# Inverting the 32 by 32 triangles of the first three time blocks as two 16 by 16 ones

## The chip, the cores and the metric

The kernel runs on one core of one Trainium2 chip. The number looked at is the device time of one execution in microseconds (us). Before the change it is 1301.52 us, the median of 3 runs that went from 1301.41 to 1301.69.

## The reference

A recurrence over 768 steps for 4 batches of 8 heads, each with a 40 by 40 state, feeds two dense layers. Its output for a step, one row per batch and step, is the input x of the layers.

```python
for t in range(S):                                   # S = 768, per batch and head
    y[:, :, t] = einsum('bhd,bhde->bhe', rt, state)
    Sa = einsum('bhde,bhe->bhd', state, at)
    state = state * wt[:, :, None, :] - einsum('bhd,bhe->bhde', Sa, bt)
    state = state + einsum('bhd,bhe->bhde', vt, kt)
x = y as (3072, 320)
h = x @ w_in;  x = (max(h, 0) + alpha * min(h, 0)) @ w_out          # 320 -> 2048 -> 320
g = x @ w_gate;  out = (silu(g) * (x @ w_val)) @ w_out2             # 320 -> 1536 -> 320
```

## The kernel before

The 768 steps are cut into 6 time blocks `m` of 128 steps, each of two chunks of 64. Within a chunk the recurrence becomes matrix products, for which a 64 by 64 unit lower triangular matrix has to be inverted for every batch, pair of heads and chunk. For one time block these are 32 triangles per 32 partitions; they lie in the tile `tt` (two tiles, used in turn by even and odd blocks).

The work has these parts. `prep_a` and `prep_b` make, batch by batch, the factors of a chunk (tiles `Wx`, `AN`, `kbt`, `KB`) and the triangles. `inverse(m)` inverts all triangles of block m. `seq` is the recurrence itself, chunk by chunk and batch by batch, two batches side by side; its first product that needs the inverse is `pp` (L731), and its multiplication by the mask is L751. `conv` turns one weight tile into 32-bit halves: three instructions on DVE (L177 to L179), one on ACT (L180), POOL's L186 and L187, a cast on ACT (L191), POOL's L192, and a store to `wd`. Its tile `wy` has one buffer, so the next tile's L177 waits for the L187 of the one before. There are 32 such tiles for the first dense layer (`c1`) and 36 for the second (`c2`). `mlp1` is the first dense layer of one time block, fed by fetches `wt<-wd`; the second layer follows at the end.

`inverse(m)` halves the 64 by 64 triangle. The two 32 by 32 diagonal blocks are inverted by forward substitution in 31 steps: each multiplies a column by a row into `tmp` (L614) and subtracts it from the rows below (L622). For the first block these columns are split in three parts, one on POOL and two on DVE; for the others in two parts on DVE. Then come two transposes on DVE (L626 into `tn`, L628 into `tt`), a product on PE (`eps`, L636), copies on ACT, and a second product (`dps`, L655) that gives the off-diagonal 32 by 32 quarter.

The order on each engine is not that of the code: a scheduler that runs when the program is built sets it, from priorities that `drive` gives as it steps several generators in proportion (`N_INV` is the number of steps that it counts for an inversion). `narrow` asks it to put POOL's L186 after the last POOL instruction of an inversion that has been recorded so far (`mark["pool"]`), where there is one. Each engine then runs its list strictly in that order, so an instruction that waits holds up all behind it.

## Time and profile before

| | us |
|---|---|
| median of 3 runs | 1301.52 |
| profiled execution, time | 1305.71 |
| profiled execution, span from first to last instruction | 1304.0 |
| PE busy | 1115.3 |
| DVE busy | 799.9 |
| ACT busy | 595.1 |
| POOL busy | 409.5 |

The profiled execution is 4.19 us longer than the median and has 1.71 us outside its span. Engines are PE (matrix products; PEld is its weight loads), DVE, ACT, POOL, and SP, which issues most transfers. Busy times add over stages with different limits, so the rows further down are taken by stage.

### The profile page before, as it was taken

To read this page: it belongs to the slowest core of one execution; us is meant where nothing else is said; L and a number is where in the kernel's file an instruction comes from. 1 tells how busy PE (TensorE), PEld (TensorE's weight loads), DVE (VectorE), ACT (ScalarE), POOL (GpSimd) and SP (SyncE) were. 2 spreads that over 40 slices of the span, in tenths; PEclk is the share of its full clock that TensorE was granted. 3 is DMA by queue.
4 is the path that set the end of the run, shared out by engine and by line. 5 is a ranking of instruction groups with operands and counts; after the bars stand their busy time and mean duration, and the time that the engine had idled before them with its cause. 6 is when DMAs were issued, how large, how long until landed. Compare 5 with 4: busy or idle time off the path is not lost.

```text
span 1304.0 us, 24772 instructions
## 1 busy us (share of the span) xinstructions
PE 1115.3 (86%) x9056; PEld 940.2 (72%) x9056; DVE 799.9 (61%) x1713; ACT 595.1 (46%) x1463; POOL 409.5 (31%) x604
## 2 busy tenths in 40 slices
PE   3522777969899988989699969999999999999998
PEld 3521667856687776777577757877888888888887
DVE  7999678899769876986987754333332323232222
ACT  4731665645673586477555453333322222222222
POOL 9886656645421353156426540000000000000000
PEclk9765779989989998999899989999999999999999
DMA  5321468876645565466648857785700000000000
GB/s 162 118 72 43 130 194 267 261 231 217 219 142 166 159 223 168 137 195 202 195 137 266 265 193 223 215 307 202 282 25 21 25 21 17 21 1 21 10 11 21
DMA packets 101128, 188.54 MB, mean 145 GB/s; under 512 B 13712, under 2 KB 43664, under 8 KB 101008
## 3 DMA queue, kind: packets, MB, share of 16 engines
q1 hardware_dynamic: 92848, 183.03, 44.1%
q10 hardware_dynamic: 8160, 3.93, 1.1%
q8 instruction: 72, 1.18, 0.4%
q14 instruction: 48, 0.39, 0.1%
HBM read 150.22 MB, written 36.70 MB: 143 GB/s over the span
## 4 chain that ended last, share of the span: by engine, by line
PE 46%; DVE 26%; DMA 12%; ACT 7%; issue 4%; POOL 3%; SPq 1%; ACTq 0%; DVEq 0%; POOLq 0%
PE pg L235 10%; PE pv L235 10%; PE u L235 5%; DMA wt<-wd 5%; DVE la L622 4%; DVE tmp L614 3%; PE o L946 3%; PE o L947 3%; PE o L945 3%; DVE AN L515 2%; PE gp L748 2%; DVE g L275 2%; PE mnp L540 2%; DMA raw_wa<-in_wa_dram 2%; DVE rest L498 2%
## 5 line engine op out<-in xcount | busy, mean ns | idle before, releaser
L191 ACT CAST gh<-g 128x512 fp32r<-128x512 f32 (+1 forms) x176 | 105.7, 600 | 184.8 <-DVE g L965 124.8
L965 DVE TENSOR_TENSOR g<-pv,sg 128x512 f32<-128x512 f32 x72 | 49.8, 692 | 227.4 <-PE pv L235 224.5
L192 DVE TENSOR_TENSOR gl<-g,gh 128x512 fp32r<-128x512 f32 (+1 forms) x176 | 123.3, 700 | 89.9 <-ACT gh L191 89.3
L235 PE MATMUL u<-xh,wt 128*128 128x512 f32 (+1 forms) x416 | 150.0, 403 | 18.8 <-DVE g L275 15.8
L275 DVE SCALAR_TENSOR_TENSOR g<-g,neg,u 128x512 f32<-128x512 f32 (+1 forms) x104 | 72.8, 700 | 71.0 <-ACT g L274 70.8
L186 POOL TENSOR_SCALAR wz<-wz 128x384 f32<-128x384 f32 (+1 forms) x68 | 79.4, 1168 | 102.6 <-ACT wz L180 74.5
L235 PEld LDWEIGHTS u<-xh,wt 128*128 128x128 f32 x416 | 79.8, 195 | 42.3 <-DVE g L275 21.8
L540 PE MATMUL mnp<-AN,kbt 128*128 128x128 f32 x384 | 67.1, 335 | 50.5 <-DVE AN L515 28.3
L963 ACT ACTIVATE sg<-pg 128x512 f32<-128x512 f32 x72 | 43.1, 599 | 139.7 <-PE pg L235 139.7
L274 ACT ACTIVATE g<-u 128x512 f32<-128x512 f32 (+1 forms) x104 | 58.8, 566 | 103.2 <-PE u L235 74.6
L235 PE MATMUL pg<-xh,wt 128*128 128x512 f32 x288 | 101.5, 392 | 0.0
L540 PEld LDWEIGHTS mnp<-AN,kbt 128*128 128x128 f32 x384 | 61.6, 244 | 54.3 <-issue 24.9
L235 PE MATMUL pv<-xh,wt 128*128 128x512 f32 x288 | 100.4, 389 | 0.0
L192 POOL TENSOR_TENSOR wc<-wz,wc 128x384 fp32r<-128x384 f32 (+3 forms) x84 | 80.8, 969 | 56.6 <-ACT wc L191 49.7
L946 PE MATMUL o<-wt,gh 128*128 128x320 f32 x288 | 87.7, 308 | 0.0
L241 PE MATMUL d<-gl,wt 128*128 128x512 f32 (+1 forms) x208 | 82.3, 398 | 6.1 <-DVE gl L192 5.8
L945 PE MATMUL o<-wt,gh 128*128 128x320 f32 x288 | 87.2, 308 | 0.0
L622 DVE TENSOR_TENSOR la<-la,tmp 128x120 f32<-128x120 f32 (+37 forms) x304 | 84.6, 307 | 1.4
L614 DVE TENSOR_TENSOR tmp<-la 128x120 f32<-128x120 f32 (+37 forms) x304 | 82.9, 300 | 2.5 <-POOL la L589 0.8
L235 PE MATMUL u<-xl,wt 128*128 128x512 f32 (+1 forms) x208 | 81.1, 390 | 1.7 <-DVE xl L192 1.7
L242 PE MATMUL d<-gh,wt 128*128 128x512 f32 (+1 forms) x208 | 78.6, 380 | 0.0
L240 PE MATMUL d<-gh,wt 128*128 128x512 f32 (+1 forms) x208 | 70.0, 397 | 8.8 <-ACT gh L191 6.7
(117 smaller groups left out, 2730.0 us busy)
## 6 DMA issues: line engine op xcount, KB each, us to landing
wt<-wd SPq DMA_DIRECT2D x128, 384.0 KB
wt<-wd SPq DMA_DIRECT2D x116, 320.0 KB
wd<-wc SPq DMA_DIRECT2D x40, 384.0 KB
raw<-in_moe_w_out_dram SPq DMA_DIRECT2D x28, 320.0 KB
wd<-wc SPq DMA_DIRECT2D x28, 320.0 KB
raw_wa<-in_wa_dram SPq DMA_DIRECT2D x48, 160.0 KB
raw_bk<-in_bk_dram SPq DMA_DIRECT2D x48, 160.0 KB
raw<-in_moe_w_in_dram SPq DMA_DIRECT2D x16, 256.0 KB
```

Of the source, the lines that this page charges most:

```text
L186: nc.gpsimd.tensor_scalar(f, f, LEAST, None, ALU.is_ge)
L191: nc.scalar.copy(out=h, in_=raw)
L192: eng.tensor_tensor(out=l, in0=raw, in1=h.bitcast(F32), op=ALU.subtract)
L235: nc.tensor.matmul(ps, lt, rh, start=(i == 0), stop=(i == len(ops) - 1))
L241: nc.tensor.matmul(ps, wh, gl, start=False, stop=False)
L242: nc.tensor.matmul(ps, wl, gh, start=False, stop=last)
L275: nc.vector.scalar_tensor_tensor(g, g, neg[:, f:f + 1], ps, ALU.mult, ALU.add)
L540: nc.tensor.matmul(ps[:, s].rearrange("p h t -> p (h t)"), kbt[:, g * SH + s].rearrange("p j t -> p (j t)"), an[:, :, g * SH + s, :],)
L614: eng.tensor_tensor(out=tv, in0=ml[:, r0:r1, kk:kk + 1].to_broadcast([128, nr, ns]), in1=tl[:, kk:kk + 1, c0:c1].to_broadcast([128, nr, ns ...
L622: last = eng.tensor_tensor(out=dst, in0=dst, in1=tv, op=ALU.subtract)
L945: nc.tensor.matmul(ops[q], gh[:, ts], wh, start=first, stop=False)
L946: nc.tensor.matmul(ops[q], gh[:, ts], wl, start=False, stop=False)
```

## The change

For blocks 0, 1 and 2 (`LASTB = 2`) `inverse` now calls `blocked`; the others call `substitute`, which is the former code of the blocks after the first. `blocked` inverts the two 16 by 16 diagonal triangles of each 32 by 32 one side by side, in 15 steps of two products and two subtractions, all on DVE. The remaining 16 by 16 quarter is made of two products on PE: `ups`, then a copy `us` on ACT, then `yps`, subtracted from `tt` on DVE. This takes three transposes in place of two: into `dn`, into `tt`, and from `tt` into `tn`. The number of steps that `drive` counts is 29 for these blocks. POOL has no part in any inversion now, so `mark["pool"]` is never set.

```diff
+QUART = 16
+LASTB = 2
+    def blocked(m, mc, ml, tl):
+        tt = mc
+        for kk in range(QUART - 1):
+            tvs = []
+            for o in (0, QUART):
+                nr, ns = QUART - 1 - kk, kk + 1
+                tmp = (mac_p if m else bp).tile([128, QUART * QUART // 4], F32, tag=f"tmp{min(o, 1)}", name="tmp")
+                tv = tmp[:, 0:nr * ns].rearrange("p (a b) -> p a b", a=nr)
+                rows, cols = slice(o + kk + 1, o + QUART), slice(o, o + kk + 1)
+                nc.vector.tensor_tensor(
+                    out=tv,
+                    in0=ml[:, rows, o + kk:o + kk + 1].to_broadcast([128, nr, ns]),
+                    in1=tl[:, o + kk:o + kk + 1, cols].to_broadcast([128, nr, ns]),
+                    op=ALU.mult,
+                )
+                tvs.append((tv, tl[:, rows, cols]))
+            for tv, dst in tvs:
+                mark["inv"] = nc.vector.tensor_tensor(out=dst, in0=dst, in1=tv, op=ALU.subtract)
+            yield
+        dn = scr(m, 0).rearrange("p (a b) -> p a b", a=NG)
+        nc.vector.transpose(out=dn.rearrange("p n s -> p s n"), in_=tl.rearrange("p t s -> p s t"))
+        yield
+        for g in range(2):
+            ups = (ps_b if m else bps).tile([128, NH, HALF], F32, tag="b" if m else f"s{2 + g}", name="ups")
+            for n in range(NH):
+                for q in range(4):
+                    nc.tensor.matmul(
+                        ups[32 * q:32 * q + 32, n, :],
+                        mc[32 * q:32 * q + QUART, g * NH + n, 0:HALF],
+                        dn[32 * q:32 * q + QUART, g * NH + n, :],
+                        tile_position=(32 * q, 32 * q),
+                    )
+            yield
+        mark["inv"] = nc.vector.transpose(out=tt[:, :, 0:HALF].rearrange("p n t -> p t n"), in_=tl)
+        yield
+        for g, ups in enumerate(upss):
+            us = (mac_p if m else bp).tile([128, NH, HALF], F32, tag="us", name="us")
+            nc.scalar.copy(out=us, in_=ups)
+            ...
+                    nc.tensor.matmul(
+                        yps[pr, n, :], us[pr, n, :], tt[pr, g * NH + n, QUART:HALF], tile_position=(32 * q, 32 * q),
+                    )
+            off = tt[:, g * NH:g * NH + NH, QUART:HALF]
+            mark["inv"] = nc.vector.tensor_tensor(out=off, in0=off, in1=yps, op=ALU.subtract)
+            yield
+        tn = scr(m, 0).rearrange("p (a b) -> p a b", a=NG)
+        mark["inv"] = nc.vector.transpose(out=tn, in_=tt[:, :, 0:HALF])
     def inverse(m):
...
+        if m > LASTB:
+            yield from substitute(m, ml, tl)
...
+        else:
+            tn = yield from blocked(m, mc, ml, tl)
-    N_PREP, N_INV, N_SEQ, N_MLP = 8, 40, 13, 2 * K1 + 4
+    def n_inv(m):
+        return 40 if m > LASTB else 29
```

How the order moves is shown at three places. The first is DVE's list where the first two inversions end. Before, the substitution of the second inversion (tiles `la_1344`, `tmp`) ends in its two transposes, and the first mask multiplication of `seq` follows at once.

```order
L179 SCALAR_TENSOR_TENSOR wy_1140<-raw_1136,wz_1141 128x384
L622 TENSOR_TENSOR la_1344<-la_1344,tmp_1839 128x10
L626 STREAM_TRANSPOSE la_1845<-la_1344 128x32x32
L628 STREAM_TRANSPOSE tt1_175<-la_1344 128x32x32
L751 TENSOR_TENSOR gs_1115<-gp_1375,mask_117 128x8x64
L177 TENSOR_SCALAR wy_1175<-raw_1173 128x320
```

Now DVE has there the transpose that ends the second substitution (L627, into `dn`), then the first inversion's transpose into `tt` (L642, tile `tt0_174`), and its two subtractions (L655) and last transpose (L658), with instructions of three weight tiles between them (L179 to L181 are the former L177 to L179).

```order
L627 STREAM_TRANSPOSE la_1802<-la_1493 128x32x32
L642 STREAM_TRANSPOSE tt0_174<-la_470 128x32x32
L179 TENSOR_SCALAR wy_1260<-raw_1256 128x384
L180 SCALAR_TENSOR_TENSOR wz_1261<-raw_1256,wy_1260 128x384
L181 SCALAR_TENSOR_TENSOR wy_1260<-raw_1256,wz_1261 128x384
L179 TENSOR_SCALAR wy_1300<-raw_1298 128x320
L180 SCALAR_TENSOR_TENSOR wz_1301<-raw_1298,wy_1300 128x320
L181 SCALAR_TENSOR_TENSOR wy_1300<-raw_1298,wz_1301 128x320
L655 TENSOR_TENSOR tt0_174<-tt0_174,yps_828 128x16x16
L179 TENSOR_SCALAR wy_1354<-raw_1350 128x384
L180 SCALAR_TENSOR_TENSOR wz_1355<-raw_1350,wy_1354 128x384
L181 SCALAR_TENSOR_TENSOR wy_1354<-raw_1350,wz_1355 128x384
```

Four more weight tiles stand between that L658 and the first mask multiplication (now L804); of the last of them, and of the second inversion's transpose into `tt1_175`, this is the end.

```order
L179 TENSOR_SCALAR wy_1518<-raw_1514 128x384
L180 SCALAR_TENSOR_TENSOR wz_1519<-raw_1514,wy_1518 128x384
L642 STREAM_TRANSPOSE tt1_175<-la_1493 128x32x32
L181 SCALAR_TENSOR_TENSOR wy_1518<-raw_1514,wz_1519 128x384
L804 TENSOR_TENSOR gs_1235<-gp_1502,mask_117 128x8x64
```

So 15 weight tiles stand ahead of the first mask multiplication where 9 stood before. The second place is PE's list there. Before, the last products of the preparations (`kbp`) are followed by `eps`, `dps` and the recurrence's `pp`.

```order
L568 MATMUL kbp<-ident,kbt 128x128 x4
L636 MATMUL eps<-la,tt_174 32x32 x64
L655 MATMUL dps<-tt_174,la 32x32 x64
L731 MATMUL pp<-tt_174,zs_166 64x64 x8
L731 MATMUL pp<-tt_174,zs_170 64x64 x8
L737 MATMUL pp<-ident,ut 128x128 x4
```

Now `ups` and `yps` of the first inversion (`tt_174`) stand ahead of `eps` (now L685), with most of the second inversion's `ups` (`tt_175`) among them.

```order
L570 MATMUL kbp<-ident,kbt 128x128 x4
L634 MATMUL ups<-la,tt_174 32x32 x128
L634 MATMUL ups<-la,tt_175 32x32 x35
L651 MATMUL yps<-tt_174,us 32x16 x64
L634 MATMUL ups<-la,tt_175 32x32 x26
L651 MATMUL yps<-tt_174,us 32x16 x64
L634 MATMUL ups<-la,tt_175 32x32 x44
L685 MATMUL eps<-la,tt_174 32x32 x64
L634 MATMUL ups<-la,tt_175 32x32 x8
L704 MATMUL dps<-tt_174,la 32x32 x64
L784 MATMUL pp<-tt_174,zs_166 64x64 x8
```

The first `pp` has moved behind 256 products of the first inversion and 113 of the second. The third place is DVE's list at the end of the third inversion (block 2, again `tt0_174`). Before, it is the substitution's last steps between instructions of `mlp1` (L275, L192) and of a weight tile.

```order
L614 TENSOR_TENSOR tmp_3918<-la_3291,la_3293 128x10
L179 SCALAR_TENSOR_TENSOR wy_2099<-raw_2095,wz_2100 128x384
L622 TENSOR_TENSOR la_3293<-la_3293,tmp_3918 128x10
L275 SCALAR_TENSOR_TENSOR g_3780<-g_3780,neg_76,u_3727 128x512
L626 STREAM_TRANSPOSE la_3924<-la_3293 128x32x32
L628 STREAM_TRANSPOSE tt0_174<-la_3293 128x32x32
```

Now the subtractions of the quarter come behind one chunk of the recurrence, and no weight tile stands near.

```order
L746 TENSOR_TENSOR ST3_182<-ST3_182,Wx_1222 128x4x40
L762 COPY gs_4072<-ST3_182 64x2x2x40 x2
L642 STREAM_TRANSPOSE tt0_174<-la_3694 128x32x32
L655 TENSOR_TENSOR tt0_174<-tt0_174,yps_4266 128x16x16
L277 SCALAR_TENSOR_TENSOR g_3763<-g_3763,neg_76,u_3728 128x512
L194 TENSOR_TENSOR gl_3767<-g_3763,gh_3766 128x512
L655 TENSOR_TENSOR tt0_174<-tt0_174,yps_4385 128x16x16
L658 STREAM_TRANSPOSE la_4462<-tt0_174 128x1024
```

Between the third inversion's first transpose (L586, now L665) and this end there were 9 weight tiles and 14 multiplications L275 before; there are 2 and 9 now. At the last chunk of the recurrence PE's list has 547 products of the first layer's second half (L240 to L246) where it had 576, and 70 groups of 8 of its first half where it had 72: this work now stands behind it.

## Rows read from the trace of the kernel before

**Rows 1.** Stages: start:end, length; busy us (instructions) by engine; PE clock; DMA.
```profile
45.40:142.00 96.60, 30.89 (x399) 28.52 (x398) 94.98 (x254) 39.63 (x107) 72.42 (x112) 0.59 0.24 79
120.40:142.00 21.60, 14.29 (x314) 12.92 (x315) 20.23 (x54) 11.83 (x26) 10.95 (x11) 0.50 0.27 87
142.00:240.00 98.00, 79.22 (x1025) 70.71 (x1023) 68.69 (x131) 64.69 (x191) 59.03 (x85) 0.85 0.66 211
240.00:320.00 80.00, 65.91 (x602) 53.90 (x601) 78.75 (x209) 38.37 (x112) 44.93 (x60) 0.96 0.76 243
320.00:800.00 480.00, 423.23 (x4438) 341.90 (x4436) 369.04 (x843) 281.45 (x731) 192.20 (x265) 0.95 0.61 191
800.00:907.00 107.00, 102.40 (x433) 80.51 (x434) 42.69 (x60) 36.59 (x62) 0.00 (x0) 1.00 0.78 253
907.00:1304.00 397.00, 391.32 (x2025) 343.91 (x2023) 110.45 (x161) 107.86 (x188) 0.00 (x0) 1.00 0.11 39
```

**Rows 2.** The chain that ends last, shares by line, from 45.4 to 142 us.
```profile
by line: DVE la L622 22.7%; DVE tmp L614 22.2%; issue 8.8%; DVE rest L498 6.8%; DVE AN L515 6.6%; DVE la L626 4.1%; DVE la L586 3.9%; DVE kbt L529 3.6%; DVE wz L178 3.4%; DVE wy L179 3.3%; DVE wy L177 2.7%; DVE tt L628 1.8%; DVE Wx L505 1.7
```

**Rows 3.** L614 alone by stage: DVE busy, then POOL busy.
```profile
45.40:142.00 96.60, 27.76 (x96) 15.14 (x31) 0.59 0.24 79
240.00:320.00 80.00, 16.70 (x52) 0.00 (x0) 0.96 0.76 243
```

**Rows 4.** L622 alone by stage, columns as in rows 3.
```profile
45.40:142.00 96.60, 27.83 (x96) 15.57 (x31) 0.59 0.24 79
240.00:320.00 80.00, 17.15 (x52) 0.00 (x0) 0.96 0.76 243
```

**Rows 5.** Groups by shape: xcount | busy us, mean ns of one | idle before.
```profile
L614 DVE TENSOR_TENSOR tmp<-la 128x21 f32<-128x21 f32 x10 | 1.9, 191 | 0.0
L614 DVE TENSOR_TENSOR tmp<-la 128x57 f32<-128x57 f32 x10 | 2.1, 209 | 0.0
L622 DVE TENSOR_TENSOR la<-la,tmp 128x60 f32<-128x60 f32 x11 | 3.6, 326 | 0.2
```

**Rows 6.** DVE in order of time: start us, us, instruction.
```profile
83.38 1.90 DVE L586 STREAM_TRANSPOSE la<-tt 128x1024 f32<-128x1024 f32 x1
...
120.36 1.96 DVE L626 STREAM_TRANSPOSE la<-la 128x1024 f32<-128x1024 f32 x1
...
141.84 0.65 DVE L751 TENSOR_TENSOR gs<-gp,mask 128x512 f32<-128x512 f32 x1
...
239.87 1.97 DVE L586 STREAM_TRANSPOSE la<-tt 128x1024 f32<-128x1024 f32 x1
...
317.27 2.21 DVE L626 STREAM_TRANSPOSE la<-la 128x1024 f32<-128x1024 f32 x1
```

**Rows 7.** PE in order of time: start us, us of all, xcount of weight-and-product pairs.
```profile
122.38 3.63 PE L636 MATMUL eps<-la,tt 32*32 32x32 f32 x128 [42.23 <-DVE la L626]
...
132.33 1.97 PE L731 MATMUL pp<-tt,zs 128*64 128x64 f32 x32 [1.18 <-POOL wc L192]
...
670.91 1.83 PE L636 MATMUL eps<-la,tt 32*32 32x32 f32 x102
```

**Rows 8.** A weight tile on DVE, in order of time.
```profile
130.51 0.33 DVE L177 TENSOR_SCALAR wy<-raw 128x320 uint32<-128x320 uint32 x1 [0.89 <-POOL wz L187]
...
135.88 0.36 DVE L177 TENSOR_SCALAR wy<-raw 128x384 uint32<-128x384 uint32 x1
...
137.45 0.55 DVE L179 SCALAR_TENSOR_TENSOR wy<-raw,wz 128x384 uint32<-128x384 uint32 x1
```

**Rows 9.** The same weight tile on POOL, in order of time.
```profile
138.73 1.17 POOL L186 TENSOR_SCALAR wz<-wz 128x384 f32<-128x384 f32 x1 [1.23 <-ACT wz L180]
139.99 1.00 POOL L187 TENSOR_TENSOR wz<-wz,wy 128x384 f32<-128x384 f32 x1
```

**Rows 10.** A piece of the chain in the first layer's last block: start, us.
```profile
816.01 1.83 PE u L235 x8
```

80 lines of the change are left out of this document (38 added, 42 removed).

## The prediction

> **What bounds the kernel now.** I read the stages first [rows 1]: which engine is full in each tells what a saved microsecond is worth there. From 907 us on PE is busy 391.32 of 397 us on the second layer, and from 800 to 907 us it is busy 102.40 of 107 while transfers run at 253 GB/s. No inversion lies there; these stages only start earlier or later. From 320 to 800 us PE is busy 423.23 of 480 us, and the blocks inverted there (3 to 5) keep their code. What changes lies before 320 us. From 45.4 to 142 us DVE is busy 94.98 of 96.6 us and PE 30.89. From 142 to 240 us no engine is full (PE 79.22, DVE 68.69 of 98). From 240 to 320 us, where the third inversion stands, DVE is busy 78.75 of 80 us and PE 65.91.
>
> Then I read the chain of the first stretch [rows 2]: the two substitution lines L622 and L614 hold 44.9% of it, all on DVE. The third reading is how much of a full DVE these lines are: 27.76 and 27.83 us in the first stretch, 96 instructions each, and 16.70 and 17.15 us in the third, 52 each [rows 3, 4]. On POOL they are another 15.14 and 15.57 us. So the change works on the right lines. The last view is what stands around the inversions in order of time [rows 6 to 9], for what is late next.
>
> **The change, part by part.** *Substitution.* A new inversion has 15 steps of 4 instructions, 60, none over 64 elements. Instructions of that size took 0.191, 0.209 and 0.326 us [rows 5]; the mean of all in the first stretch is 55.59 / 192 = 0.290. I take 0.24, between the quiet groups and the one of 60 elements, with 0.19 and 0.33 as ends. The first two inversions then take 120 x 0.24 = 28.8 us of DVE in place of 55.6, the third 14.4 in place of 33.85.
>
> *Added on DVE.* One transpose more (1.96 us, L626 in rows 6) and two subtractions of 256 elements, about half of L751's 0.65 us each: 2.6 us an inversion. POOL's loss of 30.7 us I count at nothing: no wait on it was on the chain of rows 2.
>
> *Added on PE.* `ups` and `yps` are 256 products, 512 pairs of weight load and product. `eps` ran 128 pairs in 3.63 us at granted clock 0.50, the lower of its two levels (1.2 GHz), after PE had stood idle for 42.23 us: 28 ns a pair. Late in the trace, between other work, it ran 102 in 1.83 us: 18 ns [rows 1, 7]. So 512 pairs are 14.5 us cold and 9.2 us warm. No row shows four positions of the array in turn, as these products use, only two; if four share the array as well as two do, it would be half, 4.6 to 7.3 us. I take the rows as they are. The Trainium skill speaks against a gain from this: its page "TensorE: Matmul & The Clock Gate" (section "Wait — 56ns, not 53.3ns?") says that products start no closer than about 25 ns however small they are. These 18 ns at the upper level lie below it, so the trace does not bear the floor out; by it, 512 pairs would be an estimated 12.8 us in place of 9.2.
>
> *The start of the recurrence.* DVE's content up to the first mask is 94.98 - 55.59 + 28.8 + 2.6 (the second inversion's last part stands behind the mask), plus six weight tiles more in the order (15 for 9), each 0.36 + 0.55 + about 0.55 = 1.46 us [rows 8]: 79.6 us. Seven of these tiles, three transposes and two subtractions stand behind the second inversion's L627: 10.2 + 6.6 us. So L627 ends after 62.8 us of content and the 1.6 us that DVE was idle, at about 109.8 us, and the first inversion's L642 at 111.8. Now DVE's list is a row of weight tiles, and each waits for POOL's L187 of the one before. That cycle was 135.88 - 130.51 = 5.37 us; packed, it is 1.46 on DVE, 0.73 from the end of L179 (138.00) to POOL's start (138.73), and 2.26 to the end of L187 (140.99): 4.45 us [rows 8, 9]. Six cycles, a tile and the second L642 end at 111.8 + 26.7 to 32.2 + 1.5 + 2.0: 142.0 to 147.5 us. I take 146, since the longer cycle is the one that ran. Before, L751 stood at 141.84 [rows 6]. The start is 4 us later, not earlier: the wait of `tt` and of both subtractions for the weight tiles ahead of them takes the place of the substitution.
>
> If the tiles did not hold, PE would: from 111.8, `yps` of the first half 128 x 28 ns = 3.6, a copy and the second half 4.2, subtraction and transpose 2.3, so `tn` at 121.9 where it was at 122.3, and the mask where it was; at half the price per pair, 3 us earlier. The term is +4, with -3 and +6 as ends.
>
> *From the first mask to 240 us.* Two weight tiles more stand here (15 for 13), 2.9 us on a DVE that is 70% busy, and the second inversion's `yps`, 256 x 18 ns = 4.6 us, on a PE that is 81% busy and among the recurrence's products. Idle time covers most of it: +2, from 0 to +7.
>
> *The third inversion.* Here DVE is full, and its content falls from 78.75 by 33.85 - 14.4 - 2.6 = 16.9 us, and by the seven weight tiles that are done earlier (2 in place of 9), 10.2 us: 52 us. PE is late next. Its 65.91 us grow by 9.2, and five multiplications L275 with their products stand behind the stretch now (9 for 14). Eight products of `mlp1` take 1.83 us [rows 10], and a tile of that layer has 16 of them, 3.66 us, so 18.3 us of PE work is moved back. What remains is 56.8 us; at 93% busy the stretch is 61 us: -19, from -10 (PE busy 80%) to -22.
>
> *What is moved comes back.* From 320 to 800 us PE has 56.8 us of idle time, so some of the 18.3 us is filled in there. At the last chunk of the recurrence the list is still behind by 29 products of the second half and 2 groups of 8, (29 + 16) x 0.229 = 10.3 us. I count half of the 18.3 us: +9, with 0 and +18 as ends.
>
> **Sum.** +4 + 2 - 19 + 9 = -4 us. The profiled execution took 1305.71 us, 1.71 of it outside its span, and would take 1301.7; it is 4.19 above the median, which I take over unchanged: 1297.5 us.
>
> **The rivals.** *PE takes it all back (slower).* All the moved work is paid in full, since PE is busy 88% from 320 to 800 us, and the new products as well: +4 + 2 - 19 + 18 = +5, and with the start at its upper end +7, so 1308. It is one mechanism: PE's total work grows by up to 4.6 + 9.2 us where it is loaded, and the idle time that the third stretch loses (14.1 us) pays for no more than that. It decides if PE's idle time between the first mask and 800 us falls by less than the 13.8 us of new work and the later start together, about 18 of its 89.6 us. For it speaks that DVE is not full after 320 us (369.04 of 480); against it, that PE's idle time there is three times the moved work.
>
> *Nothing remains (no change).* The start loses 6, and the third stretch gains only 14, since its chunks of the recurrence wait for each other; less is then moved, and 6 returns: +6 + 2 - 14 + 6 = 0, so 1301. For it speaks that four stretches of different limits are added here; against it, that DVE is full without a break from 240 to 320 us.
>
> *The start is not held (faster by more).* The weight tiles come at the packed cycle and cheap products bring the start to -3, and most of what is moved fits into idle time: -3 + 0 - 19 + 5 = -17, so 1284. For it speaks the POOL that is freed of 30.7 us while it feeds these tiles; against it, the 5.37 us that the cycle really took.
>
> **How the numbers follow.** About 0.2%, 2.6 us, is what a measurement of this kernel can tell from no change. My forecast of -4 and the larger gain together have 0.45 (0.30 and 0.15), no change 0.22, PE taking it all back 0.33. The forecast lies close to the bound, so these are also the chances of faster, same and slower. The range takes in most of the slower rival and the larger gain down to 1286: 1286 to 1310; the forecast's own is 1290 to 1303.
>
> **What would show it.** Substitution instructions of 0.19 to 0.29 us, 120 in the first stretch; the first mask (L804) at 142 to 148 us, behind weight tiles whose L179 waits for POOL; `ups` and `yps` at 18 to 28 ns a pair; from the third inversion's first transpose to its last one about 61 us where it was 79; PE busier than 82% there, DVE clearly less than full. I am wrong if the first mask comes before 140 us, if that stretch is over 72 us, or if PE's idle time from there to the second layer grows.

## The result and the profile after

The changed kernel takes 1315.12 us (median of 4 runs, 1312.24 to 1317.24), the kernel before 1301.61 beside it (1301.41 to 1302.5): a ratio of 1.0101, 95% interval 1.0081 to 1.0121. It is slower by 13 us; 1297.5 was predicted, and the range ended at 1310. The profiled execution of the kernel before lies 4.1 us above its median and that of the changed kernel 0.2, so the profiles show 9.5 us of the 13. Beside the experiments below, on three chips, the median of the kernel before was 1304.05 to 1306.51 us; the changed kernel was not measured there, so a few us of the 13 are not certain.

The stages of the changed kernel in the view of busy time by window; columns as in [rows 1]. The last window begins with the second layer, 9.5 us later than before:

```profile
45.40:142.00 96.60, 42.21 (x1178) 38.86 (x1179) 79.20 (x204) 46.94 (x125) 60.83 (x69) 0.58 0.36 120
142.00:240.00 98.00, 78.74 (x1219) 69.13 (x1212) 65.13 (x130) 60.15 (x177) 63.35 (x88) 0.80 0.66 213
240.00:320.00 80.00, 68.98 (x1126) 60.17 (x1125) 61.21 (x154) 38.14 (x115) 28.93 (x47) 0.88 0.57 174
320.00:800.00 480.00, 425.83 (x4439) 344.00 (x4439) 366.13 (x839) 279.45 (x728) 184.68 (x257) 0.95 0.62 191
...
916.50:1313.50 397.00, 391.36 (x2025) 343.93 (x2023) 110.48 (x161) 107.86 (x188) 0.00 (x0) 1.00 0.11 39
```

DVE is relieved as intended: 79.20 us for 94.98 in the first stretch and 61.21 for 78.75 in the third. But PE's idle time from 142 to 800 us only falls from 89.6 us [rows 1] to 19.26 + 11.02 + 54.17 = 84.5, and the granted clock is lower from 142 to 320 us (0.80 and 0.88 for 0.85 and 0.96). Over the whole kernel PE is busy 24.1 us longer (1139.4 for 1115.3) and idle 14.6 us less; the difference is the 9.5 us of the span (1313.5 for 1304.0). From the first mask to the second layer, first before and then now, the same sum is:

```profile
141.80:906.90 765.10, 670.85 (x6494) 547.12 (x6493) 559.37 (x1241) 421.00 (x1093) 296.16 (x409) 0.95 0.66 207
140.20:916.40 776.20, 687.69 (x7272) 564.12 (x7272) 537.06 (x1185) 415.92 (x1082) 278.04 (x390) 0.93 0.63 200
```

PE is busy 16.8 us longer there, of which 11.8 us are the `ups` and `yps` behind the mask and 5 us the other work, which takes longer; its idle time falls only from 94.3 to 88.5 us.

The chain that ends last, shares by line from 45.4 to 140.2 us; it answers to [rows 2]:

```profile
by line: issue 14.7%; POOL wz L188 10.3%; POOL wc L194 10.0%; POOL wz L189 9.0%; DVE tmp L615 7.9%; DVE la L623 7.3%; DVE la L665 4.0%; DVE rest L500 4.0%; ACT wc L193 3.5%; DVE AN L517 2.8%; DMA raw<-in_moe_w_in_dram 2.6%; PE gp L801 2.4%;
```

The substitution (L615, L623) has gone from 45% to 15% of it. In its place stand POOL's part of the weight tiles (L188, L189, L194, 29%) and "issue". On DVE, in order of time, one sees where (L627, L642, L655, L658 are the first inversion's end, L179 the start of a weight tile, L804 the first mask):

```profile
92.50 2.02 DVE L627 STREAM_TRANSPOSE la<-la 128x1024 f32<-128x1024 f32 x1
...
105.89 1.95 DVE L642 STREAM_TRANSPOSE tt<-la 128x1024 f32<-128x1024 f32 x1
...
112.28 0.33 DVE L179 TENSOR_SCALAR wy<-raw 128x320 uint32<-128x320 uint32 x1 [2.99 <-POOL wz L189]
...
114.33 0.41 DVE L655 TENSOR_TENSOR tt<-tt,yps 128x256 f32<-128x256 f32 x1
117.05 0.36 DVE L179 TENSOR_SCALAR wy<-raw 128x384 uint32<-128x384 uint32 x1 [2.31 <-POOL wz L189]
...
118.99 0.41 DVE L655 TENSOR_TENSOR tt<-tt,yps 128x256 f32<-128x256 f32 x1
119.44 1.25 DVE L658 STREAM_TRANSPOSE la<-tt 128x1024 f32<-128x1024 f32 x1
...
140.15 0.69 DVE L804 TENSOR_TENSOR gs<-gp,mask 128x512 f32<-128x512 f32 x1
```

From L627 to the end of L658 28.2 us pass: 13.4 before L642 starts, with the last steps of the second inversion, its own L627 and two weight tiles, and 12.8 behind L642, where weight tiles wait for POOL in front of both subtractions. The first mask comes 1.7 us earlier than L751 did [rows 6]. How the recurrence then runs is read from the masks of its 24 chunk pairs; each pair has two, one for each batch. Of the kernel before, the first mask of pair 2, both of pair 4, and the first of pairs 9, 23 and 24 (x2: both in a row):

```profile
164.88 0.69 DVE L751 TENSOR_TENSOR gs<-gp,mask 128x512 f32<-128x512 f32 x1 [0.26 <-PE gp L748]
...
205.92 0.68 DVE L751 TENSOR_TENSOR gs<-gp,mask 128x512 f32<-128x512 f32 x1
...
216.01 0.69 DVE L751 TENSOR_TENSOR gs<-gp,mask 128x512 f32<-128x512 f32 x1
...
362.14 0.69 DVE L751 TENSOR_TENSOR gs<-gp,mask 128x512 f32<-128x512 f32 x1 [2.08 <-PE gp L748]
...
766.21 1.30 DVE L751 TENSOR_TENSOR gs<-gp,mask 128x512 f32<-128x512 f32 x2
...
779.48 0.69 DVE L751 TENSOR_TENSOR gs<-gp,mask 128x512 f32<-128x512 f32 x1 [0.20 <-PE gp L748]
```

and of the changed kernel:

```profile
157.96 0.69 DVE L804 TENSOR_TENSOR gs<-gp,mask 128x512 f32<-128x512 f32 x1
...
216.15 0.68 DVE L804 TENSOR_TENSOR gs<-gp,mask 128x512 f32<-128x512 f32 x1
...
217.81 0.69 DVE L804 TENSOR_TENSOR gs<-gp,mask 128x512 f32<-128x512 f32 x1
...
357.82 1.28 DVE L804 TENSOR_TENSOR gs<-gp,mask 128x512 f32<-128x512 f32 x2
...
749.23 0.68 DVE L804 TENSOR_TENSOR gs<-gp,mask 128x512 f32<-128x512 f32 x1
...
778.58 1.28 DVE L804 TENSOR_TENSOR gs<-gp,mask 128x512 f32<-128x512 f32 x2
```

It is 1.7 us ahead at the first mask, 6.9 at pair 2, 10.2 us behind at pair 4, 4.3 ahead at pair 9, 17.0 ahead at pair 23, 0.9 ahead at the last, and the second layer begins 9.5 us late: a lead is won and spent twice. The size at one pair hangs on which mask is taken: by the second masks it is 1.8 behind at pair 4, 5.4 ahead at pair 9, 14.5 at pair 23 and 6.6 at the last. At pair 6 both agree, 8.4 and 9.0 us behind. Two windows of the changed kernel behind the first mask show PE at its lower level:

```profile
150.00:164.00 14.00, 14.00 (x250) 12.39 (x240) 6.92 (x12) 7.47 (x21) 10.26 (x13) 0.51 0.32 105
...
170.00:191.00 21.00, 14.09 (x203) 12.19 (x204) 11.77 (x22) 13.54 (x40) 9.94 (x11) 0.51 0.70 231
```

From 150 to 164 us PE is busy without a break and still runs at its lower level (1.2 GHz). But pair 2 (157.96) lies in this spell and is 6.9 us early, so the loss begins behind it, and the lower clock is not all of it. Ahead of the second spell PE stands idle, and the chain that ends last has a store of the recurrence's output there (start, us):

```profile
166.55 5.97 DMA xd<-pv
```

and on PE, in order of time (start, us, idle time before it):

```profile
173.85 1.08 PE L774 MATMUL zp<-gs,AN 128*64 128x40 f32 x16 [4.01 <-ACT s L769]
```

PE waits 4.01 us for a copy on ACT (L769), which stands in ACT's list behind another copy (L739) that waits for this store. (The kernel before has such a wait of ACT too, of 2.9 us; here it is 4.5.) And from pair 3 to pair 4 (191.37 to 216.15), with the clock at 1.00 from 195 us on, the recurrence falls a further 7.8 us back by the first masks, 3.2 by the second. No run takes these apart.

### The profile page after: what moved, and what is told of

The parts are those of the page before. It is cut to its first block, busy times and chain, and to the rows that moved or that the text cites. A ratio compares the mean times of both kernels' runs of the same rounds, so it can differ in the third digit from the quotient of the medians.

```text
span 1313.5 us, 27709 instructions
## 1 busy us (share of the span) xinstructions
PE 1139.4 (87%) x10592; PEld 963.8 (73%) x10592; DVE 761.5 (58%) x1606; ACT 596.6 (45%) x1469; POOL 378.6 (29%) x542
## 4 chain that ended last, share of the span: by engine, by line
PE 47%; DVE 18%; DMA 12%; ACT 11%; issue 5%; POOL 5%; SPq 1%; ACTq 0%; POOLq 0%; DVEq 0%
PE pg L237 10%; PE pv L237 10%; PE u L237 6%; PE o L999 3%; PE o L1000 3%; PE o L998 3%; DMA wt<-wd 3%; DMA xd<-pv 3%; DMA raw_wa<-in_wa_dram 2%; PE gp L801 2%; POOL wz L188 2%; PE d L242 1%; DVE gs L762 1%; DVE g L277 1%; PE d L243 1%
## 5 line engine op out<-in xcount | busy, mean ns | idle before, releaser
L237 PE MATMUL u<-xh,wt 128*128 128x512 f32 (+1 forms) x416 | 154.4, 412 | 26.2 <-DVE g L277 15.4
L194 DVE TENSOR_TENSOR gl<-g,gh 128x512 fp32r<-128x512 f32 (+1 forms) x176 | 122.0, 693 | 88.7 <-ACT gh L193 88.1
L237 PEld LDWEIGHTS u<-xh,wt 128*128 128x128 f32 x416 | 82.6, 202 | 48.9 <-DVE g L277 19.8
L188 POOL TENSOR_SCALAR wz<-wz 128x384 f32<-128x384 f32 (+1 forms) x68 | 80.8, 1188 | 75.5 <-ACT wz L182 53.0
L542 PE MATMUL mnp<-AN,kbt 128*128 128x128 f32 x384 | 62.5, 317 | 46.0 <-DVE AN L517 16.5
L194 POOL TENSOR_TENSOR wc<-wz,wc 128x384 fp32r<-128x384 f32 (+3 forms) x84 | 80.1, 961 | 69.1 <-ACT wc L193 63.4
L542 PEld LDWEIGHTS mnp<-AN,kbt 128*128 128x128 f32 x384 | 56.2, 224 | 50.7 <-issue 20.8
L1000 PE MATMUL o<-wt,gl 128*128 128x320 f32 x288 | 76.9, 309 | 0.0
L755 POOL COPY gs<-raw_v 64x160 f32<-64x160 f32 x96 | 40.2, 419 | 124.2 <-DVE tmp L595 36.0
```

What stands on the lines that cost most here:

```text
L188: nc.gpsimd.tensor_scalar(f, f, LEAST, None, ALU.is_ge)
L194: eng.tensor_tensor(out=l, in0=raw, in1=h.bitcast(F32), op=ALU.subtract)
L237: nc.tensor.matmul(ps, lt, rh, start=(i == 0), stop=(i == len(ops) - 1))
L542: nc.tensor.matmul(ps[:, s].rearrange("p h t -> p (h t)"), kbt[:, g * SH + s].rearrange("p j t -> p (j t)"), an[:, :, g * SH + s, :],)
L1000: nc.tensor.matmul(ops[q], gl[:, ts], wh, start=False, stop=last)
```

## The experiments

Four theories were set against each other. (P): the new products cost their time on a PE that is the limit. (W): the weight tiles in the first inversion's way are to blame. (O): the scheduler's order is, not the instructions. (C): PE spends more time at its lower clock. "Lower clock" below is twice (1 - granted clock) times the length, added over twenty equal windows from 45.4 us to the second layer's first product; it is in microseconds. Times within a kernel are of its one profiled execution, which can lie far from the median: 1325.78 us for 1312.78 in e3_wait0, 1326.41 for 1316.89 in e5_hold01_fac, 1312.43 for 1317.54 in e4_b_seq; elsewhere they are within 4.2 us. Ratios are to runs of the kernel before on the same chip. One table for all:

| kernel | first mask | second layer | lower clock | ratio (95%) |
|---|---|---|---|---|
| before | 141.8 | 906.9 | 161 | 1 |
| changed | 140.2 | 916.4 | 192 | 1.0101 (1.0081 to 1.0121) |
| e1_block2 | 143.7 | 915.6 | 183 | 1.0068 (1.0045 to 1.0092) |
| e1_blocks01 | 142.0 | 921.1 | 201 | 1.0096 (1.0064 to 1.0128) |
| e1_noprod | 123.0 | 892.8 | 156 | 0.9865 (0.9833 to 0.9897) |
| e1_twice | 159.5 | 973.4 | 273 | 1.0462 (1.0388 to 1.0536) |
| e2_hold | 135.4 | 927.4 | 216 | 1.0132 (1.0100 to 1.0163) |
| e2_noprod2 | 142.2 | 921.3 | 199 | 1.0125 (1.0102 to 1.0147) |
| e2_hold01 | 134.8 | 909.6 | 170 | 1.0049 (1.0032 to 1.0066) |
| e2_pace | 143.5 | 912.2 | 165 | 1.0066 (1.0041 to 1.0092) |
| e3_noprod1 | 141.1 | 924.5 | 200 | 1.0143 (1.0123 to 1.0163) |
| e3_wait012 | 128.0 | 923.6 | 198 | 1.0125 (1.0100 to 1.0151) |
| e3_wait0 | 130.9 | 926.9 | 210 | 1.0050 (1.0030 to 1.0070) |
| e4_b_fac | 144.5 | 901.6 | 150 | 0.9951 (0.9926 to 0.9977) |
| e4_b_seq | 141.3 | 913.6 | 175 | 1.0079 (1.0058 to 1.0101) |
| e4_a_pace | 142.9 | 932.6 | 208 | 1.0169 (1.0127 to 1.0211) |
| e4_a_fac | 143.1 | 908.3 | 168 | 1.0018 (0.9991 to 1.0044) |
| e5_a_seq | 141.9 | 914.2 | 191 | 1.0077 (1.0053 to 1.0101) |
| e5_hold01_fac | 136.2 | 927.2 | 195 | 1.0108 (1.0069 to 1.0148) |

**Parts of the change: e1_block2 and e1_blocks01.**

```diff
-        if m > LASTB:
-            yield from substitute(m, ml, tl)
+        if m not in BLOCKED:        # {2}, and {0, 1}
+            ...                     # the substitution of the kernel before
```

> Only the third time block is inverted by quarters; the first two are inverted as in the kernel before, POOL's share of them included. Four theories. (P) PE pays: PE limits the stretch from the first mask to 907 us, so every product added there is paid (11.55 us of ups and yps stand after 142 us in the changed kernel, 7.2 of them in the third inversion), and the idle time saved is small: about 1301.6 + 7 less a few us of idle time that the third stretch loses, 1304 to 1309, and the granted clock as before up to 240 us. (W) The weight tiles that move ahead of and between the parts of the first inversions are to blame: then this kernel does not lose, 1290 to 1302. (O) The scheduler lets the recurrence run ahead of the first layer after a quicker third inversion and pays at the end: most of the loss is here, 1310 to 1316. (C) The granted clock, lower by 0.05 to 0.08 from 142 to 435 us, is the loss and comes from the new front: the clock is as before here and the time 1290 to 1302.

> The first two time blocks are inverted by quarters, the third by substitution as in the kernel before. (P) 4.4 us of products stand after the first mask, and the recurrence starts about 2 us earlier: 1302 to 1306. (W) The order of weight tiles in the front is as in the changed kernel: all of the loss is here, 1311 to 1316. (O) No loss: the third stretch is as long as before, 1299 to 1303. (C) The clock falls from 142 to 320 us as in the changed kernel (0.80 and 0.88 where it was 0.85 and 0.96), and the time is 1308 to 1316.

Each part loses, 0.7% and 1.0%, and together they lose no more than the second. No theory had both. (W) alone falls with e1_block2, which has the front of before and still loses; the third block's quicker inversion won nothing by itself. Each of the two losses is no larger than what the order alone can do (below), so neither is firm.

**The products: e1_noprod and e1_twice.**

```diff
-            for n in range(NH):
+            for n in range(1):                                     # e1_noprod; the n for both us and off is 0
+            for n in [n for n in range(NH) for _ in range(2)]:     # e1_twice
                 for q in range(4):
```

> As the changed kernel, but of the 256 ups and 256 yps products of each of the three inversions only the 4 of the first n of each half are computed, 16 in place of 512; the copy to us and the subtraction read that one n for all, in their full length, so the lower left quarter is not what it should be. DVE and ACT do as much as in the changed kernel. (P) PE loses 24 us of work, 11 of them after the first mask: at least those 11 us come back, 1298 to 1304, and less if the front is shorter as well. (W) and (O) The order of weight tiles and the quicker inversions stay: the loss stays, 1310 to 1316. (C) If the small products hold the clock down, it rises to 0.85 and 0.96 from 142 to 320 us and the time falls to about 1300; if the idle time ahead of them does, clock and time stay.

> As the changed kernel, but each ups and yps product is issued twice in a row, to the same place with the same values: 25 us more of PE work, 13.7 of them before 142 us and 11.5 after it. (P) The 11.5 us are paid in full, and of the first 13.7 those on the chain to the first mask: 1327 to 1340, the first mask 3 to 7 us later. (W), (O) and (C) The products lie in PE's idle time (84 us from 142 to 800 us), so little is added: 1315 to 1321.

Without the products the kernel is 1.35% faster than before and 2.4% faster than the changed one, which is 31 us; with twice as many it is 3.6% slower than the changed one, 47 us. Both differences are larger than the 20 us between the fastest and the slowest order of the changed kernel (the order alone, below). (P) is right in kind and too small in size: 1536 weight-and-product pairs more cost 47 us, 31 ns each, where it had 28 cold and 18 warm, and far more than the 16 ns of busy time that PE shows for one (25.3 us for 1536). Of the 24 us by which e1_noprod's second layer begins earlier than in the changed kernel, 17 are there at the first mask; from there to the second layer it takes 769.8 us, 6.5 fewer than the changed kernel and still 4.8 more than the kernel before (765.0). DVE at the first inversion's end in e1_noprod, to be set beside the changed kernel's rows above:

```profile
94.97 2.00 DVE L627 STREAM_TRANSPOSE la<-la 128x1024 f32<-128x1024 f32 x1
97.95 1.91 DVE L642 STREAM_TRANSPOSE tt<-la 128x1024 f32<-128x1024 f32 x1
100.66 0.42 DVE L655 TENSOR_TENSOR tt<-tt,yps 128x256 f32<-128x256 f32 x1
...
102.33 1.25 DVE L658 STREAM_TRANSPOSE la<-tt 128x1024 f32<-128x1024 f32 x1
```

8.6 us in place of 28.2. But the scheduler, which counts fewer products, has also put fewer weight tiles and fewer steps of the second inversion in between; the next kernel takes the tiles out alone.

**Weight tiles out of the way: e2_hold and e2_hold01** (the second with the third block as before).

```diff
+    c1 = after(mark['inv'], c1)
     rest1 = chain(p1, inverse(1))
```

> As the changed kernel, but the weight tiles of the first phase that are emitted behind the first inversion wait for its last transpose (L658), so none stands between L627 and L658 in DVE's order; the products stay. (W) In the changed kernel 26.9 us pass from L627 (92.50) to the end of L658 (120.7), with four weight tiles between them, while PE is busy 12 us of it; without products the same stretch took 8.6 us and held one tile. If the tiles hold it, it falls to 9 to 14 us, the first mask comes at 122 to 130 us, and the time falls by 10 to 18 us against the changed kernel: a ratio to before of 0.996 to 1.003. (P) If the products hold it, the stretch stays over 20 us, the mask at 136 us or later, and the time at a ratio of 1.005 to 1.012.

> As e2_hold, and the third block is inverted by substitution as before, so the first two blocks alone are changed. (W) The mask comes as in e2_hold, 122 to 130 us. (P) Without the 7.2 us of products in the third stretch, but with its 17 us of DVE back: within 4 us of e2_hold on either side. (C) The stretch from 142 to 240 us has the clock of the changed front, 0.80 or less, whatever the third block does.

DVE at the same place in e2_hold:

```profile
95.22 2.04 DVE L627 STREAM_TRANSPOSE la<-la 128x1024 f32<-128x1024 f32 x1
102.67 2.02 DVE L627 STREAM_TRANSPOSE la<-la 128x1024 f32<-128x1024 f32 x1
104.53 1.92 DVE L642 STREAM_TRANSPOSE tt<-la 128x1024 f32<-128x1024 f32 x1
110.10 0.42 DVE L655 TENSOR_TENSOR tt<-tt,yps 128x256 f32<-128x256 f32 x1 [3.65 <-PE yps L651]
116.28 0.42 DVE L655 TENSOR_TENSOR tt<-tt,yps 128x256 f32<-128x256 f32 x1 [5.75 <-PE yps L651]
116.73 1.25 DVE L658 STREAM_TRANSPOSE la<-tt 128x1024 f32<-128x1024 f32 x1
```

No tile stands there, and it still takes 22.8 us, so of the 28.2 us (26.9 in the expectation, which ends at the start of L658) the tiles held 5.4. The second L627 is the second inversion's: from the first L627 to L642 DVE works without a break on that inversion's last steps, 9.3 us where e1_noprod takes 3.0. Behind L642 the subtractions now wait for PE, 3.65 and 5.75 us, and from the end of L642 to the end of L658 it is 11.5 us, where e1_noprod takes 3.7 and the changed kernel, with its tiles, 12.8. So the products hold that part nearly as long without the tiles as the tiles do with them. (W)'s 9 to 14 us and its mask at 122 to 130 us failed; (P)'s stretch of over 20 us held, with the mask 0.6 us too early for it. The 4.8 us won at the mask were lost again: the second layer begins 11 us later than in the changed kernel in these two executions, and the medians (1.0132 for 1.0101) are not told apart. e2_hold01 loses 0.5%, less than e2_hold by more than (P)'s 4 us, although its clock from 142 to 240 us is 0.78, as low as (C) had said.

**The products of one inversion: e2_noprod2 and e3_noprod1.** The edit of e1_noprod, for `m == 2` and for `m == 1` alone.

> As the changed kernel, but in the third inversion alone only 4 products in place of 128 are computed for each half of ups and yps, so the quarter there is not what it should be; copies and subtractions keep their length. Up to 250 us every engine has the order of the changed kernel. (P) 7.2 us of products less where PE limits: first mask at 140 us, mask to second layer 776 less 6 to 8, 768 to 770 us; ratio to before about 1.004. (O) The order of the recurrence ahead of the first layer is the loss, products or not: 774 to 778 us. (C) If the small products pull the clock down from 284 to 332 us (0.88 there as a mean), it is at 0.95 or above there and 10 to 14 us come back.

> As the changed kernel, but in the second inversion alone only 4 products in place of 128 are computed for each half of ups and yps, so the quarter there is not what it should be; copies and subtractions keep their length. In the changed kernel the granted clock fell at 150.6 us while PE was busy, in the midst of the second inversion's yps among the recurrence's products, and stayed low to 163.6 us, and again from 170.8 to 191 us. (C) Those products pull the clock down: without them it is at 0.84 or above as a mean of the 100 us behind the first mask (0.79 in the changed kernel, 0.85 before), and mask to second layer falls from 776 to 764 to 770 us. (P) They cost their 4.4 us: 771 to 773 us, and the clock stays at 0.80. (O) Nothing: 776 us.

Both are as slow as the changed kernel or slower. (P)'s 4 to 8 us did not come back, and (C)'s higher clock did not come either (0.82 in the 100 us behind the mask of e3_noprod1, where 0.84 was the least it allowed; 0.89 from 284 to 332 us in e2_noprod2, where it asked for 0.95). That the time after the mask hangs on the products of the second or of the third inversion by itself is not shown. It is not refuted either, since the scheduler orders these kernels anew, and the order alone moves a kernel by as much (below).

**PE alone: e3_small.** A kernel with nothing but PE loops of each shape:

```diff
+    warm(48)                                  # 128x512
+    for k in range(1024):
+        nc.tensor.matmul(ups[p, n, :], tt[h, n, :], la[h, n, :], tile_position=(32 * q, 32 * q))
+    warm(48)
+    ...                                       # 1024 as yps, 768 as eps, 96 of 128x128
```

> No kernel of the reference: the output is left at zero. PE alone runs, in a row: 1024 products of the shape of ups (16 by 32 with 16 by 32, four positions in turn), 1024 of the shape of yps (32 by 32 with 32 by 16, four positions), 768 of the shape of eps (32 by 32, two positions), 96 of 128 by 128, and 48 of 128 by 512 before, between and behind them. (C) The clock is at its upper level in the wide products and falls within a stretch of small ones though PE never stops: a mean of 0.6 to 0.8 there; then a pair of four positions costs about 15 to 25 ns and one of two 28 ns. (P), (O) and (W): the clock stays at 0.95 or above in all stretches, 18 ns a pair or less for two positions and about 10 for four.

PE in order of time in the stretch shaped like `ups`, then in the one shaped like `eps` (start, us, records; each product of 32-bit floats is two records):

```profile
40.80 1.93 PE L120 MATMUL ups<-la,tt 16*32 16x32 f32 x128 [1.80 <-issue]
44.81 1.93 PE L120 MATMUL ups<-la,tt 16*32 16x32 f32 x128 [2.07 <-issue]
...
159.20 3.09 PE L130 MATMUL eps<-la,tt 32*32 32x32 f32 x183
162.98 3.42 PE L130 MATMUL eps<-la,tt 32*32 32x32 f32 x128 [0.69 <-issue]
...
174.17 17.99 PE L130 MATMUL eps<-la,tt 32*32 32x32 f32 x640 [0.38 <-issue]
```

PE does 128 pairs of four positions in 1.93 us, 15 ns each, and then stands for 1.5 to 2.1 us with nothing to do but "issue". From the group at 25.89 us to that at 70.91 us it is 3.75 us for 128 in the mean (3.45 to 4.01), 29.3 ns a pair. The reason is read from the page's part on DMA queues, here of e3_small, where PE has 6064 pairs:

```profile
q8 instruction: 47, 0.77, 1.4%
```

47 packets for 6064 pairs are 128 pairs to a packet. The kernel before has 72 such packets, the changed one 84 (twelve more for 1536 pairs more), e1_twice 96. PE's instructions come in packets of 128 pairs, one in 3.75 us here, and a dense row of small products waits for them whatever it would take on the array: two groups that ran at the upper level for all or most of their time, 128 in 1.27 us at 22.16 us and 128 in 1.34 us at 94.07 us, were each followed by the next only 3.73 us after their start. The two-position products of [rows 7] took 28 ns on the array and hid this. In the full kernel less of this is seen: PE's idle time put down to "issue" ahead of `ups` and `yps` is 8.6 us in the changed kernel and 19.6 us in e1_twice, 11 of the 57 us between their profiled spans, where PE's busy time grows by 40 (1139.4 to 1179.7). So that a pair costs 31 ns there, near the 29 ns of the packets, is in the main not their doing. The windows of the same kernel show the clock (PE, weight loads, DVE, POOL, then clock, DMA):

```profile
7.50:18.60 11.10, 11.04 (x48) 8.93 (x48) 0.01 (x1) 0.00 (x0) 1.00 0.83 354
26.00:76.00 50.00, 26.05 (x1746) 24.35 (x1748) 0.00 (x0) 0.00 (x0) 0.50 0.02 4
168.00:171.00 3.00, 3.00 (x120) 3.00 (x117) 0.00 (x0) 0.00 (x0) 0.50 0.00 0
174.00:202.00 28.00, 26.74 (x962) 26.09 (x962) 0.00 (x0) 0.00 (x0) 0.50 0.02 5
...
216.00:234.00 18.00, 18.00 (x164) 18.00 (x163) 0.00 (x0) 0.00 (x0) 1.00 0.00 1
```

Wide products hold the upper level, and so do those of 128 by 128. The small ones do not: the `eps` stretch begins at the upper level with 183 pairs in 3.09 us, 17 ns each, stops for 0.69 us, and then runs at 28 ns at the lower level, with PE busy 26.74 of 28 us and for 3 us without any break. The clock of (C) was right here (0.50 even, where it had 0.6 to 0.8), and the price of 15 to 29 ns with it. "Though PE never stops" was not: rows of small products had stops for instructions, the 128 by 128 ones had none, and this kernel does not tell whether the level falls for the stops or for the smallness.

**The first inversion alone: e3_wait012 and e3_wait0** (the second with the first block alone by quarters).

```diff
+    c1 = after(mark['inv'], c1)
-    rest1 = chain(p1, inverse(1))
+    rest1 = chain(p1, after(mark['inv'], inverse(1)))
```

> As the changed kernel, but the second inversion, and the weight tiles of the first phase emitted behind the first inversion, wait for the first inversion's last transpose, so that it runs alone on DVE and PE. (W) and (P) The first inversion's substitution is no longer shared with the second's, and no product of the second stands between its own: its last transpose comes at 95 to 105 us in place of 119.4, the first mask at 116 to 126 us in place of 140.2. (C) The second inversion moves whole behind the first mask, with all of its 512 products: the clock in the 100 us behind it is 0.80 or less, and mask to second layer grows to 780 us or more, so that the time is 1295 to 1312. (P) The 4 us of ups behind the mask are added: 776 + 4 = 780 and the time 1292 to 1300.

> As e3_wait012, but the first block alone is inverted by quarters; the second waits as there and goes by substitution, as does the third. The first mask as there, 116 to 126 us. (C) No small products of ups and yps stand behind the first mask: the clock in the 100 us behind it is 0.84 or above and mask to second layer is 765 to 772 us, so the time is 1280 to 1292, the first kernel here that beats the one before. (P) The same within 2 us. (O) The order decides: no telling, 1285 to 1305.

The mask came 12 and 9 us earlier than in the changed kernel, short of what was expected, and in these executions none of it was left at the end: 795.6 and 796.0 us from mask to second layer, where the kernel before takes 765.0 (that of e3_wait0 lies 13 us above its median). Starting the recurrence earlier is not worth that time by itself. e3_wait0 did not beat the kernel before (0.5% slower), outside the range of every theory. The clock speaks against (C) as well: in the 100 us behind the mask it is 0.85 in e3_wait012, with 512 small products there, where 0.80 or less was expected, and 0.72 in e3_wait0, which has no `ups` and `yps` there, where 0.84 or more was.

**The order alone: e2_pace, e4_b_fac, e4_b_seq on the kernel before; e4_a_pace, e4_a_fac, e5_a_seq on the changed one.** One number in the interleaving, and no instruction more or less:

```diff
-    N_PREP, N_INV, N_SEQ, N_MLP = 8, 40, 13, 2 * K1 + 4
+    N_PREP, N_INV, N_SEQ, N_MLP = 8, 29, 13, 2 * K1 + 4      # e2_pace; e4_a_pace: n_inv returns 40
+    N_PREP, N_INV, N_SEQ, N_MLP = 8, 40, 14, 2 * K1 + 4      # e4_b_seq; e5_a_seq likewise
-FAC = 1.0
+FAC = 1.1                                                    # e4_b_fac, e4_a_fac
```

> The kernel before with one number changed: an inversion counts 29 steps in place of 40 where the steps of the recurrence, the inversion and the first layer are interleaved. No instruction is added or taken away, only the order moves. It tells how much the order alone is worth. (O) If the order alone can lose what the changed kernel lost, the time is 5 us or more away from that before, on either side. (P), (W) and (C) say nothing of it; if it lies within 3 us, a difference of 10 us is no accident of the order.

> The kernel before with the inversion's share of the interleaving raised from 1.0 to 1.1; no instruction is added or taken away, the front up to the first mask keeps its order. (O) If the order of the kernel before is a lucky one among many alike, this loses 3 to 12 us against it, as e2_pace did (8 us). (C) and (P) The same time within 3 us, and PE at its lower level from 45.4 us to the second layer for 150 to 165 us, as before (157).

> The kernel before with a block of the recurrence counted as 14 steps in place of 13 in the interleaving; no instruction is added or taken away. As e4_b_fac: (O) a loss of 3 to 12 us, (C) and (P) within 3 us. What orders of the kernel before cost on the whole is read from e2_pace, e4_b_fac and e4_b_seq together.

> The changed kernel with all inversions counted as 40 steps in the interleaving, as in the kernel before; no instruction is added or taken away. (O) Such changes move the changed kernel by up to 8 us to either side, 1303 to 1323, and its orders lie on the whole within 3 us of the orders of the kernel before. (C) Every order of the changed kernel has 25 us or more of lower clock beyond the orders of before, and lies 5 to 15 us above them. (P) 6 to 12 us above them, with the same lower clock.

> The changed kernel with the inversion's share of the interleaving raised from 1.0 to 1.1; no instruction is added or taken away. As e4_a_pace: (O) 1303 to 1323 and the mean of the orders of the changed kernel within 3 us of that of before; (C) 5 to 15 us above it with 25 us or more of lower clock; (P) 6 to 12 us above it without.

> The changed kernel with a block of the recurrence counted as 14 steps in the interleaving, as e4_b_seq did it in the kernel before; no instruction is added or taken away. Ratios so far, with the same number in both: 1.0101 to 1 as they stood, 1.0018 to 0.9951 with the inversion's share at 1.1, and 1.0169 with 40 steps. (O) The two groups overlap: 0.998 to 1.008 here, at or below the 1.0079 of e4_b_seq. (C) and (P) The change costs its 6 to 10 us in any order: 1.012 to 1.018. (C) alone: the second layer begins at 161 us of lower clock plus half a us for each further one, 906.9 + 0.56 x (low - 161), within 5 us, as in the kernels so far.

The order alone moves the kernel before from 0.9951 to 1.0079 and the changed one from 1.0018 to 1.0169. The groups overlap. Their means over four orders each are 1.0024 and 1.0091: 0.67% apart, about 9 us, with a standard error of 0.43% from their spreads (0.60% and 0.62%), so that anything from 5 us faster to 22 us slower is possible. With the same number in both, the changed kernel was slower by 0.7% (FAC 1.1), by 1.0% (as given; 1.7% where both count 40 steps), and equal (14 steps for the recurrence). e4_b_fac, the kernel before with FAC 1.1, is the fastest that computes everything: 0.9951, faster than both kernels. It also failed every theory: (O) had expected a loss, (C) and (P) no change. e4_a_pace lost more than any had allowed, e4_a_fac less than (C) and (P) had, and e5_a_seq fell where (O) had put it.

**The earlier start in the better order: e5_hold01_fac.** e2_hold01 with `FAC = 1.1`.

> e2_hold01 (the first two blocks inverted by quarters, weight tiles behind the first inversion's last transpose) with the inversion's share of the interleaving at 1.1, which took 6 us off the kernel before and 11 off the changed one. (O) The gains of the order and of the earlier start add: 1.0049 less 0.005 to 0.008, 0.997 to 1.000, not better than e4_b_fac at 0.9951. (C) and (P) The same, and any order that has more than 160 us of lower clock up to the second layer is slower than the kernel before.

The gains did not add: 1.0108 where 0.997 to 1.000 was expected, and (O) failed here as a rule of sums.

**What goes with the time.** Over the 19 kernels of the table the second layer begins at about 812 us + 0.56 x the lower clock (correlation 0.96; 0.47 and 0.92 without e1_twice). About half a microsecond for each one at half the clock is what a full PE would lose. It is not exact: e5_a_seq, by 906.9 + 0.56 x 30 to be at 923.7, was at 914.2, and the 5 us set for it failed. It is a connection across kernels and not a test by itself, since a longer kernel has more time to be slow in; that rows of small products run at the lower level is shown by e3_small, that they are the cause of the spells in the full kernel is not, and e3_wait0 has the lowest clock without them.

## Why the prediction was wrong

The step that failed is the overlap behind the first mask: "Idle time covers most of it" was said of the work added from there to 240 us, and the term was +2, from 0 to +7. By pair 6 (260 to 275 us), the first behind this stretch where both masks agree, the recurrence had lost 10 to 11 us. What the runs show in place of the overlap is the sum from the first mask to the second layer: PE was busy 16.8 us longer and idle only 5.7 us less. The cause of the 5 us that the other work took longer, and of the waits in this stretch, stays open. None of the three signs by which the prediction would have known itself wrong came up: the first mask stood at 140.15 us, the third stretch took 62.2 us, and PE's idle time fell. Part by part:

- *Substitution.* 0.24 us an instruction was taken; it was (12.84 + 13.96) / 120 = 0.223 in the first stretch, from these rows of L615 and L623 that answer to [rows 3, 4]:

```profile
45.40:142.00 96.60, 12.84 (x60) 0.58 0.36 120
...
45.40:142.00 96.60, 13.96 (x60) 0.58 0.36 120
```

- *Added on PE.* 28 ns and 18 ns a pair were taken, and half of that named as the other possibility. On the array it is about half, 244 pairs of `ups` in 3.51 us at the lower clock, 14.4 ns:

```profile
94.58 3.51 PE L634 MATMUL ups<-la,tt 16*32 16x32 f32 x244 [18.37 <-DVE la L627]
99.93 0.42 PE L634 MATMUL ups<-la,tt 16*32 16x32 f32 x12 [1.84 <-issue]
```

  The second row shows what undoes it: 1.84 us of "issue", PE out of instructions. In a dense row the price is 29 ns at either level (e3_small). The value for cold products was right for a reason that the prediction did not have; that for warm ones, 18 ns, is too low in a dense row and too high between other products, where 52 pairs of `yps` took 0.63 us at 146.76 us, 12 ns each. The 25 ns that the Trainium skill gives as the least distance of products (page "TensorE: Matmul & The Clock Gate", section "Wait — 56ns, not 53.3ns?") are not a floor in these 244 either; what holds them apart over a longer row is the 29 ns of the packets.
- *The start of the recurrence.* +4 was taken with -3 as an end, and -1.7 came. That tiles waiting for L189 stand ahead of the subtractions was right, with cycles near 5 us (112.28 to 117.05). But e2_hold shows that they held only 5.4 of the 28.2 us. PE's chain, which the prediction had put second at 10.1 us from the end of L642 to `tn` (111.8 to 121.9), took 11.5 us in e2_hold. POOL, which it counted at nothing, holds 29% of the chain of this stretch now with its part of the tiles (the line of [rows 2] breaks off at 1.7%; the chain before held 3.2 us of POOL behind that).
- *From the first mask to 240 us.* +2 was taken, with +7 as the end. From the first mask to pair 6 the recurrence lost 10.1 us by the first masks (1.7 ahead to 8.4 behind) and 10.9 by the second. "Idle time covers most of it" counted work against idle time and left out that PE might do the same work more slowly, and that what waits in one engine's list holds the others: PE's clock was 0.58 from 150 to 191 us, where it had been 0.80, and it stood 4.0 us behind ACT's wait for a store. How much each of these cost is not shown. This step failed.
- *The third inversion.* 61 us were expected from the first transpose to the last; 62.2 came, from 252.54 to the end of L658 at 314.72, where it was 79.6:

```profile
252.54 1.93 DVE L665 STREAM_TRANSPOSE la<-tt 128x1024 f32<-128x1024 f32 x1
...
313.47 1.25 DVE L658 STREAM_TRANSPOSE la<-tt 128x1024 f32<-128x1024 f32 x1
```

  The recurrence won 12.7 us from pair 6 to pair 9, the first that this inversion feeds (14.4 by the second masks), where -19 was taken, with -10 and -22 as ends (80% busy gives 56.8 / 0.80 = 71 us, so -9 and not -10). DVE's side of the change did what was said of it.
- *What is moved comes back.* +9 was taken, half of the moved work, with +18 as the end. From pair 9 to the second layer the 4.3 us of lead became 9.5 us of lateness: 13.8 us came back (14.9 by the second masks), inside the ends and 5 us more than was taken. On the way the lead grew to 17.0 us at pair 23 and was lost again. The terms as measured: -1.7 + 10.1 - 12.7 + 13.8 = +9.5 by the first masks, -1.9 + 10.9 - 14.4 + 14.9 = +9.5 by the second; +4 + 2 - 19 + 9 was taken.

The rival "PE takes it all back" was the right one by its own condition: PE's idle time fell by 5 us (89.6 to 84.5), where less than 18 was its mark. Its sum was another: of the 18.3 us of moved work 13.8 came back, and the larger loss lay ahead of the third inversion. It priced the case at 1308, too low, as it had neither the lower clock (192 us for 161 up to the second layer) nor the packets. What the prediction left out of its terms altogether is the order: e2_pace lost 0.66% and e4_b_fac won 0.49% with the same instructions, so any edit that makes the scheduler lay the work anew carries about 8 us of chance, the spread of these orders, larger than the whole forecast of -4. How much of the 13 us belongs to the change in every order and how much to the order it got is open: about 9 us by the means, with the wide bounds above. That the products are the costly part of the change is shown (31 us between e1_noprod and the changed kernel, 47 to e1_twice), and that 17 of the 24 us in the profiles of e1_noprod are won ahead of the first mask; where in the kernel they cost time after the mask is not, since leaving out those of one inversion gave nothing back. An experiment with the same order and other products could not be made, as the scheduler lays the order by the products it sees.

## What to carry to other kernels

Microseconds taken from an engine that is full only in places are worth what the engine that limits the end loses of idle time; PE's idle time before and after, stage by stage, is the sum to make first, and the time at its lower clock the second. Work handed to PE as many small products costs, in a dense row, a supply of instructions, here 29 ns a pair and two pairs a product, and not the array time that its busy column shows; between other work it cost more than its own busy time here as well, through order and clock, in shares that stayed open. Where a scheduler orders the work, try a few neutral orders of both kernels before a difference of one per cent is put down to an edit.

## What the runs showed of the hardware

- PE's instructions arrived in packets of 128 weight-and-product pairs, one in 3.75 us in the mean in a dense row (29 ns a pair); the packets of queue q8 count them: 47 for 6064 pairs, 72 and 84 in the kernels before and after.
- Four positions of the array in turn took 14.4 to 15 ns a pair at 1.2 GHz, about half of the two positions' 28 ns.
- In a row of 32 by 32 products PE fell to 1.2 GHz after a stop of 0.69 us and stayed there while it was busy 26.74 of 28 us; 128 by 128 products, without stops, held 2.4 GHz.
